# Feed-forward stages 1 to 3 in products of 512 and 384 tokens instead of twice 448

## The chip, the cores and the metric

The kernel runs on one core of a Trainium2 chip. A core has a matrix engine (TensorE, PE in the profile; its weight loads are listed apart as PEld), three engines for elementwise work (VectorE = DVE, ScalarE = ACT, GpSimd = POOL) and a queue engine for transfers (SyncE = SP). They run their own instruction streams and wait for each other by semaphores. The metric is the device time of one execution in microseconds, the median of several.

## The reference

Attention with 2 batches, 12 heads, 448 tokens, head size 64, with a causal mask, and on its output two feed-forward layers with 896 tokens, model width 768 and inner width 2048:

```python
scores = scale * np.matmul(q, k.transpose(0, 1, 3, 2))      # masked above the diagonal, softmax
x = attention_output.transpose(0, 2, 1, 3).reshape(896, 768)
h = x @ w_in;   g = h * np.cos(h);    x = g @ w_out          # layer 1
h = x @ w_in2;  g = gate(h);          out = g @ w_out2       # layer 2
# gate(h): h where h >= 1, 0 where h <= -1, else (h + 1)**2 / 4
```

The weights reach the kernel as 64-bit floats, which it reads as integer words.

## The kernel before, in words

**The four feed-forward products are stages.** Stage 1 is x1 @ w_in, stage 2 is g1 @ w_out, stage 3 is x2 @ w_in2, stage 4 is g2 @ w_out2. Every factor is split into a high and a low part in the format fp32r (`whi`, `wlo`, `x1h`, `x1l`, ...), and each product is the sum of three passes: high by high, low of the activations, low of the weights (`passes`).

**In stages 1 to 3 the weights are stationary and the tokens move.** A matmul loads 128x128 weights into the array and streams tokens past them. All 896 tokens don't fit one matmul, since one writes into one bank of PSUM, 512 fp32 wide. The kernel before streams the two batches apart, 448 tokens each, into a tile `m` of two banks of which it uses the first 448 columns each: `ps[:, b, :S]`.

**A unit** is one piece of weights that is loaded by one DMA, decoded and used: 66 in all. In stage 1 and 3 a unit is a column block of 128 with 6 chunks of the contraction (`c`), so 6 chunks x 2 batches x 3 passes = 36 matmuls (line 442), in the order batch, chunk, pass. In stage 2 an output block takes three units of 5, 5 and 6 chunks (`f`), 30, 30 and 36 matmuls (line 471), in the order chunk, batch, pass. Stage 1 has 16 units, stage 2 has 18, stage 3 has 16. Stage 4 turns the roles round: activations stationary, 384 weight columns moving (line 578), 16 units of 42 matmuls.

**Work beside the matmuls.** `ahead(u)` issues, after the matmuls of unit u, the decode of unit u+2 (lines 143 to 167, on ACT and DVE, the last step writes `wlo`) in turns with the activation of unit u (`act_cos`, lines 353 to 366, in stage 1; `act_gate`, lines 372 to 382, in stage 3; `act_none`, lines 385 and 387, after an output block of stage 2). The activation reads the finished `m` as `[128, 2, 448]` and writes the high and low part of the next stage's factor. Four `m` tiles take turns. Stage 3 begins with five of its six chunks, and only then needs the last block of x2, whose activation runs meanwhile: the first unit sorts its matmuls so that chunk 5 comes last, and runs the rest of the activation (`before`) ahead of it.

**Attention ends before stage 1 does its own.** Parts of units 0 and 1 (60 of their 72 matmuls) fill holes at the end of the attention (`FILL`, `ffn_in_part`). The order on each engine is the order in which the code issues: the schedule is written by hand.

Of the kernel before, what the change touches and what calls it, by code (L numbers as in the profile page):

```python
# [60 lines left out]
def attention_then_two_ffn(  # L61
# [17 lines left out]
    nc = tc.nc  # L79
    B, H, S, D = shape  # L80
    NT, DM = out.shape
    DFF = w_in1.shape[1]
    NP = H // 2
    KD = DM // P
# [18 lines left out]
    def f32(t):  # L103
        return t.bitcast(F32)
# [14 lines left out]
    raws, ready = {}, {}  # L119
# [264 lines left out]
    def act_none(h, xh, xl):  # L384
        nc.scalar.copy(out=xh, in_=h)
        yield
        nc.vector.tensor_tensor(out=xl, in0=h, in1=f32(xh), op=ALU.subtract)


    def joint(t):  # L390
        return t.rearrange("p (b s) -> p b s", b=B)

    def run(gen):
        if gen is not None:
            next(gen, None)
# [4 lines left out]
    def decode(u):  # L400

        if u < len(units):
            if u not in decodes:
                decodes[u] = decode_unit(u)
            run(decodes[u])

    def ahead(u, act=None):

        now, late, work["now"] = work["now"], work["late"], act
        d = u + W_AHEAD
        run(late)
        decode(d)
        run(now)
        run(now)
        decode(d + 1)
        decode(d)
        run(now)
        run(now)  # L420
        decode(d)
        decode(d)
        run(now)
        work["late"] = now

    def passes(w, x):
        return ((w[0], x[0]), (w[0], x[1]), (w[1], x[0]))

    parts = {}

    def ffn_in_part(u, x, b, chunks):

        if u not in parts:
            parts[u] = (new_ps(), ready.pop(u), set())
        ps, w, done = parts[u]
        s = slice(b * S, (b + 1) * S)
        for c in chunks:
            first = not any((b, i) in done for i in range(KD))
            done.add((b, c))
            last = all((b, i) in done for i in range(KD))  # L440
            for t, (l, r) in enumerate(passes(w, x)):
                nc.tensor.matmul(  # L442
                    ps[:, b, :S], l[:, c, :], r[c][:, s], start=(first and t == 0), stop=(last and t == 2)
                )

    def ffn_in(u, x, g, act, before=None):

        for fc in range(KF):
            done = parts[u][2] if u in parts else set()
            left = [(b, c) for b in range(B) for c in range(KD) if (b, c) not in done]  # L450
            if fc == 0:
                left.sort(key=lambda bc: (bc[1] == KD - 1, bc))
            for b, c in left:
                if c == KD - 1 and before:
                    before()
                    before = None
                ffn_in_part(u, x, b, (c,))
            ps = parts.pop(u)[0]
            ahead(u, act(ps[:, :, :S], joint(g[0][fc]), joint(g[1][fc]), u))
            u += 1  # L460

    def ffn_mid(u, g, x):
        for dc in range(KD):
            ps = new_ps()
            for f0, m in MID:
                w = ready.pop(u)
                for f in range(m):
                    for b in range(B):
                        s = slice(b * S, (b + 1) * S)
                        for t, (l, r) in enumerate(passes(w, g)):  # L470
                            nc.tensor.matmul(  # L471
                                ps[:, b, :S], l[:, f, :], r[f0 + f][:, s],
                                start=(f0 + f == 0 and t == 0), stop=(f0 + f == KF - 1 and t == 2),
                            )
                ahead(u)
                u += 1
            last = act_none(ps[:, :, :S], joint(x[0][dc]), joint(x[1][dc]))
            if dc < KD - 1:
                work["now"] = last
        return last  # L480
# [16 lines left out]
    def new_ps():  # L497
        made.append(None)
        return ps_m[(len(made) - 1) % 4].tile([P, 2, 512], F32, tag="s", name=f"m{len(made)}")
# [55 lines left out]
    ps_m += [ps_2, ps_2]  # L555
    g1 = new_g("g1")
    ffn_in(0, x1, g1, act_cos)
    x2 = new_x("x2")
    last = ffn_mid(KF, g1, x2)
    g2 = new_g("g2")  # L560
    u = KF + KD * len(MID)
    ffn_in(u, x2, g2, act_gate, lambda: [run(last), run(last)])
    u += KF


    TB = NT // P
    for e in range(2):
        po = []
        for t in range(0, TB, 2):
            ps = new_ps()  # L570
            po += [ps[:, i, :NO] for i in range(2)]
        for f0 in range(0, KF, 2):
            w = ready.pop(u)
            for t in range(TB):
                s = slice(t * P, (t + 1) * P)
                for f in range(2):
                    for i, (r, l) in enumerate(passes(w, g2)):
                        nc.tensor.matmul(  # L578
                            po[t], l[f0 + f][:, s], r[:, f, :],
                            start=(f0 + f == 0 and i == 0), stop=(f0 + f == KF - 1 and i == 2),  # L580
                        )
            ahead(u)
            u += 1
        for t in range(TB):
            ob = x_p.tile([P, NO], F32, tag=f"x{'hl'[e]}{t % KD}", name=f"ob{e}_{t}")
            if t % 2:
                nc.vector.tensor_copy(out=ob, in_=po[t])
            else:
                nc.scalar.copy(out=ob, in_=po[t])
            nc.sync.dma_start(out=out[t * P : (t + 1) * P, e * NO : (e + 1) * NO], in_=ob)  # L590
# [31 lines left out]
```

## Time and profile before

| | us |
|---|---|
| median of 3 runs | 566.83 (566.78 to 567.08) |
| the profiled execution, as a run | 566.84 |
| its span in the trace | 565.0 |
| stage 1 without fill, from its unit 2: first matmul | 102.55 |
| stage 2 begins | 206.71 |
| stage 3 begins | 325.75 |
| stage 4 begins | 444.79 |
| last matmul of stage 4 begins | 561.10 |

The profiled execution lies on the median, so its rows can be summed against it. The 1.8 us between span and run lie outside the trace.

Matmuls are pipelined: the time that a row gives as the duration of one holds its way through the array, and the next begins long before it ends. What a matmul costs in a stream of its kind is the distance from its start to the start of the next.

### The profile page before, as it was taken

What the parts mean: (1) busy time and instruction counts of PE and PEld (TensorE: products, weight loads), DVE (VectorE), ACT (ScalarE), POOL (GpSimd) and SP (SyncE); (2) the same over time, 40 slices, a digit from 0 to 9 for tenths busy, and PEclk for the clock granted to TensorE, in tenths of its full rate; (3) what the DMA queues carried; (4) which work ended last, traced back from release to release, by engine and by line L of the source; (5) the groups of instructions that cost most, each with busy time, mean ns of one, the idle gap of its engine ahead of it and who ended that gap; (6) DMA issues with size and microseconds to landing.
All of it is one profiled execution on the core that took longest, in us unless ns stands there. A gap on an engine that the chain in (4) does not pass through costs nothing.

```text
span 565.0 us, 8048 instructions
## 1 busy us (share of the span) xinstructions
PE 557.9 (99%) x3105; PEld 495.6 (88%) x3105; DVE 398.7 (71%) x566; ACT 291.7 (52%) x477; POOL 55.1 (10%) x106
## 2 busy tenths in 40 slices
PE   7999999999999999999999999999999999999997
PEld 3666678999999999999999999999999999999997
DVE  5777574699999997654754678888889875547501
ACT  4998883777777773322222245556555622232101
POOL 4657662000000000000000000000000000000000
PEclk9999999999999999999999999999999999999999
DMA  9843011233333324332423523333334343354002
GB/s 311 292 140 98 2 57 33 80 112 113 112 113 102 103 93 150 103 102 94 148 65 104 169 66 105 109 113 111 113 112 113 99 128 114 108 162 160 1 1 98
DMA packets 49254, 62.25 MB, mean 110 GB/s; under 512 B 1856, under 2 KB 43584, under 8 KB 49216
## 3 DMA queue, kind: packets, MB, share of 16 engines
q1 hardware_dynamic: 49072, 61.51, 34.5%
q8 instruction: 24, 0.39, 0.3%
q10 hardware_dynamic: 144, 0.23, 0.1%
q14 instruction: 14, 0.11, 0.1%
HBM read 58.98 MB, written 2.75 MB: 109 GB/s over the span
## 4 chain that ended last, share of the span: by engine, by line
PE 98%; DVE 1%; ACT 0%; issue 0%; POOL 0%; ACTq 0%; POOLq 0%
PE m L442 42%; PE m L471 21%; PE m L578 21%; PE o L334 4%; PE sa L219 2%; PE tx L309 2%; PE sc L206 2%; PE tw L309 1%; PE tz L309 1%; PE sb L219 1%; PE warm L513 1%; DVE nma L247 0%; ACT p L269 0%; PE sa L229 0%; PE sa L232 0%
## 5 line engine op out<-in xcount | busy, mean ns | idle before, releaser
L164 ACT CAST whi<-f 128x768 fp32r<-128x768 f32 (+1 forms) x66 | 54.0, 818 | 119.5 <-DVE f L157 78.5
L167 DVE TENSOR_TENSOR wlo<-f,whi 128x768 fp32r<-128x768 f32 (+1 forms) x63 | 58.4, 928 | 47.7 <-ACT whi L164 47.7
L578 PE MATMUL m<-whi,g2h 128*128 128x384 f32 x224 | 74.8, 334 | 0.0
L578 PE MATMUL m<-wlo,g2h 128*128 128x384 f32 x224 | 74.8, 334 | 0.0
L578 PE MATMUL m<-whi,g2l 128*128 128x384 f32 x224 | 74.8, 334 | 0.0
L442 PE MATMUL m<-x1h,whi 128*128 128x448 f32 x192 | 70.9, 369 | 0.0
L442 PE MATMUL m<-x2l,whi 128*128 128x448 f32 x192 | 70.7, 368 | 0.0
L471 PE MATMUL m<-g1h,wlo 128*128 128x448 f32 x192 | 70.7, 368 | 0.0
L442 PE MATMUL m<-x2h,wlo 128*128 128x448 f32 x192 | 70.7, 368 | 0.0
L471 PE MATMUL m<-g1l,whi 128*128 128x448 f32 x192 | 70.7, 368 | 0.0
L442 PE MATMUL m<-x2h,whi 128*128 128x448 f32 x192 | 70.7, 368 | 0.0
L471 PE MATMUL m<-g1h,whi 128*128 128x448 f32 x192 | 70.7, 368 | 0.0
L442 PE MATMUL m<-x1h,wlo 128*128 128x448 f32 x192 | 70.7, 368 | 0.0
L442 PE MATMUL m<-x1l,whi 128*128 128x448 f32 x192 | 70.6, 368 | 0.0
L143 ACT ACTIVATE f<-raw 128x768 f32<-128x768 f32 (+1 forms) x66 | 58.7, 891 | 20.9 <-DVE wlo L167 20.9
L157 DVE SCALAR_TENSOR_TENSOR f<-raw,f 128x768 uint32<-128x768 uint32 (+1 forms) x66 | 61.8, 936 | 2.3
L154 DVE SCALAR_TENSOR_TENSOR f<-raw,f 128x768 uint32<-128x768 uint32 (+1 forms) x66 | 61.4, 930 | 0.9
L578 PEld LDWEIGHTS m<-whi,g2h 128*128 128x128 f32 x224 | 42.1, 188 | 0.0
L578 PEld LDWEIGHTS m<-whi,g2l 128*128 128x128 f32 x224 | 42.1, 188 | 0.0
L578 PEld LDWEIGHTS m<-wlo,g2h 128*128 128x128 f32 x224 | 42.0, 188 | 0.0
L442 PEld LDWEIGHTS m<-x2l,whi 128*128 128x128 f32 x192 | 36.0, 188 | 3.7
L471 PEld LDWEIGHTS m<-g1h,wlo 128*128 128x128 f32 x192 | 36.0, 188 | 3.7
(91 smaller groups left out, 912.9 us busy)
## 6 DMA issues: line engine op xcount, KB each, us to landing
raw<-in_moe_w_in SPq DMA_DIRECT2D x32, 768.0 KB, 4.5
raw<-in_moe_w_out SPq DMA_DIRECT2D x22, 768.0 KB, 4.4
raw<-in_moe_w_out SPq DMA_DIRECT2D x12, 640.0 KB, 3.8
v<-in_v SPq DMA_DIRECT2D x12, 256.0 KB, 5.0
k<-in_k SPq DMA_DIRECT2D x12, 224.0 KB, 4.7
out<-ob SPq DMA_DIRECT2D x14, 192.0 KB, 1.9
qr<-in_q SPq DMA_DIRECT2D x11, 224.0 KB, 4.9
qr<-in_q ACTq DMA_DIRECT2D x1, 224.0 KB, 3.6
```

Of the source, the lines that this page charges most:

```text
L143: nc.scalar.activation(out=fl, in_=raw.bitcast(F32).rearrange("p (m two) -> p m two", two=2)[:, :m, 1], func=AF.Abs)
L154: nc.vector.scalar_tensor_tensor(out=bits, in0=low, scalar=29, in1=bits, op0=ALU.logical_shift_right, op1=ALU.bitwise_or,)
L157: nc.vector.scalar_tensor_tensor(out=bits, in0=high, scalar=0xC0000000, in1=bits, op0=ALU.bitwise_and, op1=ALU.bitwise_or,)
L164: nc.scalar.copy(out=hi[:, :m], in_=fl)
L167: e.tensor_tensor(out=lo[:, :m], in0=fl, in1=f32(hi)[:, :m], op=ALU.subtract)
L206: nc.tensor.matmul(s[heads(j), :S], self.q[heads(j), FULL * QB :], self.k[heads(j), :], start=True, stop=False)
L219: nc.tensor.matmul(s[:, j, o : o + w], self.q[heads(j), i * QB : w], self.k[heads(j), :w], start=(o == 0), stop=False,)
L309: nc.tensor.transpose(o, i, ident)
L334: nc.tensor.matmul(self.o[heads(j), c * QB : S], self.v[:, j, c, :], self.pT[:, c, j, c * QB :], start=(c == 0), stop=(c == FULL),)
L442: nc.tensor.matmul(ps[:, b, :S], l[:, c, :], r[c][:, s], start=(first and t == 0), stop=(last and t == 2))
L471: nc.tensor.matmul(ps[:, b, :S], l[:, f, :], r[f0 + f][:, s], start=(f0 + f == 0 and t == 0), stop=(f0 + f == KF - 1 and t == 2),)
L578: nc.tensor.matmul(po[t], l[f0 + f][:, s], r[:, f, :], start=(f0 + f == 0 and i == 0), stop=(f0 + f == KF - 1 and i == 2),)
```

## The change

Tokens are no longer cut at the batch border but after 512. A unit of stages 1 to 3 does all its matmuls on one of the two spans, 512 or 384 tokens, and then all on the other; the next unit begins with the span with which the last one ended (`spans.reverse()`). The tile `m` is used flat, columns 0 to 895 over both banks, and read by the activations as two times 448 columns of that. Units 0 and 1, which are begun during the attention, stay with 448. The first unit of stage 3 still keeps chunk 5 for its end, first of the 384 span, then of the 512 span.

```diff
+    spans = [slice(0, 512), slice(512, NT)]
+
+    def flat(ps):
+        return ps.rearrange("p b s -> p (b s)")[:, :NT]
...
     def ffn_in(u, x, g, act, before=None):
         for fc in range(KF):
-            done = parts[u][2] if u in parts else set()
-            left = [(b, c) for b in range(B) for c in range(KD) if (b, c) not in done]
-            if fc == 0:
-                left.sort(key=lambda bc: (bc[1] == KD - 1, bc))
-            for b, c in left:
...
-                ffn_in_part(u, x, b, (c,))
-            ps = parts.pop(u)[0]
-            ahead(u, act(ps[:, :, :S], joint(g[0][fc]), joint(g[1][fc]), u))
+            if u in parts:
+                done = parts[u][2]
+                for b in range(B):
+                    ffn_in_part(u, x, b, [c for c in range(KD) if (b, c) not in done])
+                h = parts.pop(u)[0][:, :, :S]
+            else:
+                h, w = flat(new_ps()), ready.pop(u)
+                left = [(s, c) for s in spans for c in range(KD)]
+                if before:
+                    left = [(s, c) for s in spans for c in range(KD - 1)] + [(s, KD - 1) for s in spans[::-1]]
+                for s, c in left:
...
+                    for t, (l, r) in enumerate(passes(w, x)):
+                        nc.tensor.matmul(
+                            h[:, s], l[:, c, :], r[c][:, s],
+                            start=(c == 0 and t == 0), stop=(c == KD - 1 and t == 2),
+                        )
+                if left[-1][0] is not spans[0]:
+                    spans.reverse()
+                h = joint(h)
+            ahead(u, act(h, joint(g[0][fc]), joint(g[1][fc]), u))
...
     def ffn_mid(u, g, x):
-            ps = new_ps()
+            ps = flat(new_ps())
...
-                for f in range(m):
-                    for b in range(B):
-                        s = slice(b * S, (b + 1) * S)
+                for s in spans:
+                    for f in range(m):
                         for t, (l, r) in enumerate(passes(w, g)):
                             nc.tensor.matmul(
-                                ps[:, b, :S], l[:, f, :], r[f0 + f][:, s],
+                                ps[:, s], l[:, f, :], r[f0 + f][:, s],
...
+                spans.reverse()
                 ahead(u)
-            last = act_none(ps[:, :, :S], joint(x[0][dc]), joint(x[1][dc]))
+            last = act_none(joint(ps), joint(x[0][dc]), joint(x[1][dc]))
```

On PE in the first unit of stage 2 the kernel before issues this; `m_2282` is the sum's tile, `g1h_1382` and `g1h_1383` the high parts of the activations of chunks 0 and 1 (`g1l` the low ones), `whi_2207` and `wlo_2208` the unit's weights:

```order
1063 L471 MATMUL m_2282<-g1h_1382,whi_2207 128x448
1064 L471 MATMUL m_2282<-g1l_1398,whi_2207 128x448
1065 L471 MATMUL m_2282<-g1h_1382,wlo_2208 128x448
1066 L471 MATMUL m_2282<-g1h_1382,whi_2207 128x448
1067 L471 MATMUL m_2282<-g1l_1398,whi_2207 128x448
1068 L471 MATMUL m_2282<-g1h_1382,wlo_2208 128x448
```

And the changed kernel, on PE in the middle of the same unit, where the width changes (chunk 4 is `g1h_1386`):

```order
1075 L489 MATMUL m_2282<-g1h_1386,whi_2207 128x512
1076 L489 MATMUL m_2282<-g1l_1402,whi_2207 128x512
1077 L489 MATMUL m_2282<-g1h_1386,wlo_2208 128x512
1078 L489 MATMUL m_2282<-g1h_1382,whi_2207 128x384
1079 L489 MATMUL m_2282<-g1l_1398,whi_2207 128x384
1080 L489 MATMUL m_2282<-g1h_1382,wlo_2208 128x384
```

The second batch of a chunk, which followed the first at once, has moved behind all chunks of the first span: fifteen matmuls of 512, then fifteen of 384, as many as before.

On PE at the end of the first unit of stage 3 the kernel before has its six matmuls of chunk 5 (`x2h_2275`, `x2l_2281`) in one width:

```order
1669 L442 MATMUL m_3132<-x2h_2275,whi_3048 128x448
1670 L442 MATMUL m_3132<-x2l_2281,whi_3048 128x448
1671 L442 MATMUL m_3132<-x2h_2275,wlo_3049 128x448
1672 L442 MATMUL m_3132<-x2h_2275,whi_3048 128x448
1673 L442 MATMUL m_3132<-x2l_2281,whi_3048 128x448
1674 L442 MATMUL m_3132<-x2h_2275,wlo_3049 128x448
1675 L442 MATMUL m_3183<-x2h_2270,whi_3096 128x448
```

The changed kernel has there:

```order
1669 L471 MATMUL m_3132<-x2h_2275,whi_3048 128x384
1670 L471 MATMUL m_3132<-x2l_2281,whi_3048 128x384
1671 L471 MATMUL m_3132<-x2h_2275,wlo_3049 128x384
1672 L471 MATMUL m_3132<-x2h_2275,whi_3048 128x512
1673 L471 MATMUL m_3132<-x2l_2281,whi_3048 128x512
1674 L471 MATMUL m_3132<-x2h_2275,wlo_3049 128x512
1675 L471 MATMUL m_3183<-x2h_2270,whi_3096 128x512
```

Chunk 5 stands at the same places, 31st to 36th of the unit, and the next unit goes on with 512. Over the whole program 1656 matmuls of 448 have become 828 of 512 and 828 of 384, the width changes 50 times, and the rows of the other engines and of the DMA queues are the same in the same order.

## Rows read from the trace of the kernel before

**Rows 1.** The page: busy time of the engines, and the clock granted to PE.

```profile
PE 557.9 (99%) x3105; PEld 495.6 (88%) x3105; DVE 398.7 (71%) x566; ACT 291.7 (52%) x477; POOL 55.1 (10%) x106
...
PEclk9999999999999999999999999999999999999999
```

**Rows 2.** The page: the chain of work that ended last.

```profile
PE 98%; DVE 1%; ACT 0%; issue 0%; POOL 0%; ACTq 0%; POOLq 0%
PE m L442 42%; PE m L471 21%; PE m L578 21%; PE o L334 4%; PE sa L219 2%; PE tx L309 2%; PE sc L206 2%; PE tw L309 1%; PE tz L309 1%; PE sb L219 1%; PE warm L513 1%; DVE nma L247 0%; ACT p L269 0%; PE sa L229 0%; PE sa L232 0%
```

**Rows 3.** The timeline of PE where stages meet: start us, us, engine, line, operation.

```profile
206.71 0.37 PE L471 MATMUL m<-g1h,whi 128*128 128x448 f32 x1
...
325.75 0.37 PE L442 MATMUL m<-x2h,whi 128*128 128x448 f32 x1
...
444.58 0.37 PE L442 MATMUL m<-x2h,wlo 128*128 128x448 f32 x1
444.79 0.34 PE L578 MATMUL m<-whi,g2h 128*128 128x384 f32 x1
444.97 0.33 PE L578 MATMUL m<-whi,g2l 128*128 128x384 f32 x1
445.14 0.33 PE L578 MATMUL m<-wlo,g2h 128*128 128x384 f32 x1
...
561.10 0.34 PE L578 MATMUL m<-wlo,g2h 128*128 128x384 f32 x1
```

**Rows 4.** The timeline of PE, a burst of fill matmuls between attention's.

```profile
88.30 0.37 PE L442 MATMUL m<-x1l,whi 128*128 128x448 f32 x1
...
89.11 0.37 PE L442 MATMUL m<-x1h,wlo 128*128 128x448 f32 x1
```

**Rows 5.** The timeline of DVE in stage 1: two rounds of the write of `wlo`.

```profile
107.52 0.95 DVE L167 TENSOR_TENSOR wlo<-f,whi 128x768 fp32r<-128x768 f32 x1
...
113.55 1.08 DVE L362 TENSOR_TENSOR ax<-m,ar 128x896 f32<-128x896 f32 x1
114.55 0.95 DVE L167 TENSOR_TENSOR wlo<-f,whi 128x768 fp32r<-128x768 f32 x1
```

**Rows 6.** The timeline of PE: the first matmul of unit 3.

```profile
109.99 0.37 PE L442 MATMUL m<-x1h,whi 128*128 128x448 f32 x1
```

**Rows 7.** The timeline of ACT: reading `m`, and a read of SBUF beside it.

```profile
150.67 0.91 ACT L353 ACTIVATE ax<-m 128x896 f32<-128x896 f32 x1
151.61 0.95 ACT L354 ACTIVATE ar<-ax 128x896 f32<-128x896 f32 x1
```

**Rows 8.** The timeline of DVE: the last low parts of g1 and of x2.

```profile
213.82 1.09 DVE L366 TENSOR_TENSOR g1l<-ax,g1h 128x896 fp32r<-128x896 f32 x1
...
326.89 1.09 DVE L387 TENSOR_TENSOR x2l<-m,x2h 128x896 fp32r<-128x896 f32 x1 [5.10 <-ACT x2h L385]
```

**Rows 9.** Groups of weight loads, 92 to 445 us: count, busy us, mean ns, idle before.

```profile
L471 PEld LDWEIGHTS m<-g1h,whi 128*128 128x128 f32 x192 | 36.0, 188 | 3.5
```

More of the change, by code (lines that the diff above doesn't have):

```diff
@@ L448, in ffn_in @@
         for fc in range(KF):
-            done = parts[u][2] if u in parts else set()
-            left = [(b, c) for b in range(B) for c in range(KD) if (b, c) not in done]
-            if fc == 0:
-                left.sort(key=lambda bc: (bc[1] == KD - 1, bc))
-            for b, c in left:
-                if c == KD - 1 and before:
-                    before()
-                    before = None
-                ffn_in_part(u, x, b, (c,))
-            ps = parts.pop(u)[0]
-            ahead(u, act(ps[:, :, :S], joint(g[0][fc]), joint(g[1][fc]), u))
+            if u in parts:
[9 more added lines that the diff above has]
+                for s, c in left:
+                    if c == KD - 1 and before:
+                        before()
+                        before = None
+                    for t, (l, r) in enumerate(passes(w, x)):
[7 more added lines that the diff above has]
+            ahead(u, act(h, joint(g[0][fc]), joint(g[1][fc]), u))
             u += 1
```

## The prediction

> **What bounds the kernel now.** First the page's busy times and the clock. PE is busy 99% of the span at its higher level, 2.4 GHz, from end to end [rows 1]. The chain that ended last is 98% PE; lines 442, 471 and 578, the four feed-forward stages, hold 84% of the span [rows 2]. So a nanosecond off each matmul of stages 1 to 3 comes off the end, as long as nobody else gets late. What one costs has to be read from starts, not from durations (0.37 us each, overlapping). Between the stage borders of the timeline [rows 3] lie:
> - stage 2: 576 matmuls of 448 in 325.75 - 206.71 = 119.04 us, 206.67 ns each; stage 3: 576 in 444.79 - 325.75 = 119.04 us, the same. No wait is in either: two stages with different engines busy beside them agree to the nanosecond.
> - stage 4: 671 steps of 384 columns in 561.10 - 444.79 = 116.31 us, 173.3 ns each.
>
> At one column per cycle of 2.4 GHz these would be 186.67 and 160.0 ns. So a matmul of 448 pays 20.0 ns over its columns, one of 384 pays 13.3 ns. The change lives on what one of 512 pays.
>
> **The change, part by part.**
>
> *The widths.* 1656 matmuls of 448 become 828 of 512 and 828 of 384; columns, weight loads and count stay. A pair costs 2 x 206.67 = 413.33 ns before. After it costs P(384) + P(512). For P(384) the nearest row is stage 4's 173.3 ns: same format, same 128x128 weight load, though there the activations are stationary. With it, break-even is P(512) = 240.0 ns. No row has a 512 of this format, so I bound it:
> - Low: the 13.3 ns of the 384 is a fixed price, and the 448 pays 6.7 more for being no whole number of 128 columns. P(512) = 213.33 + 13.3 = 226.7 ns; the pair saves 13.3 ns.
> - Middle: the price grows in steps, 13.3 for 3 x 128 columns, 20.0 for anything above 384. P(512) = 213.33 + 20.0 = 233.3 ns; the pair saves 6.67 ns. The three prices would be 2, 3 and 3 times 6.67 ns, one for each border between blocks of 128 columns that the stream passes. The same value comes from adding 64 columns at the clock, 26.67 ns, to the nearest row, the 448.
> - High: the straight line through both rows, (206.67 - 173.33)/64 = 0.521 ns a column, gives 206.67 + 33.33 = 240.0 ns and no gain. Above it, if the price grows by half each 64 columns (13.3, 20, 30), stand 243.3 ns and a loss of 3.3 ns a pair.
>
> I take the middle: 448 is the nearest row in width and in the roles of the operands. One row says that the 20 ns are not rigid: in a short burst between attention's matmuls the same form took (89.11 - 88.30)/4 = 202.5 ns [rows 4]. So part of the price is a phase between weight load and stream and not the stream itself; from there P(512) would be 202.5 + 26.67 = 229.2, between low and middle. Gain: 828 x 6.67 = 5.52 us.
>
> *The changes of width.* There are 50 instead of the one at stage 4's door. That one shows its price: the first 384 after a 448 lasted 444.97 - 444.79 = 0.18 us against 0.173 in the stream [rows 3], some 6 ns. 49 x 6 = 0.3 us to pay; bounds 0 and 0.6. Had the widths alternated from matmul to matmul, 1656 such changes would have cost 9.9 us; grouped, this term is small whatever the direction.
>
> *The weight loads.* A load is listed with 188 ns [rows 9], longer than 173 ns. Stage 4 streams 384 columns behind each load at 173.3 all the same, so a short matmul does hide a load, and its price is in the row. Nothing added.
>
> *Cover on DVE in stage 1.* DVE is the tightest neighbour. Its round lasts 114.55 - 107.52 = 7.03 us there [rows 5], and PE's unit 36 x 206.67 = 7.44 us. Unit 3's `wlo` is ready at 107.52 + 0.95 = 108.47 and first wanted at 109.99 [rows 6]: 1.52 us to spare, growing by 0.41 a unit. After, the unit takes 18 x 406.67 = 7.32 us, at the low bound 7.20: the reserve still grows, by 0.29 or 0.17. Cost nothing. In stages 2 and 3 the reserve is larger.
>
> *Reading `m` flat.* The activations now read two times 448 columns across the bank border. Reading `m` takes ACT 0.91 us, a like operation on SBUF 0.95 [rows 7]: 896 elements set the time, no bank shows. Zero; 0.1 us more for each of the two DVE readings would make the DVE round 7.23, still under 7.32.
>
> *The order inside a unit.* In the third unit of stage 2, chunk 15 of g1 is wanted after 15 matmuls rather than 30. Its low part ends at 214.91 [rows 8]; the unit begins near 219.1 in the old trace (60 matmuls after 206.71) and wants it at 222.2. Seven microseconds of room. The last block of x2 ends at 326.89 + 1.09 = 327.98 [rows 8] and is wanted 30 matmuls into stage 3: before at 325.75 + 6.20 = 331.95, after 6.10 instead of 6.20 behind the door, 3.9 us of room. Both zero; should either cover go, it would be paid once.
>
> **Sum.** 566.84 - 5.52 + 0.29 = 561.6 us. The profiled execution is on the median, so this stands for the median too.
>
> **Rivals.**
>
> *The price is a straight line, or a price of the place.* Then cutting 896 columns as 512 + 384 or 448 + 448 is the same. Two mechanisms lead there: 0.521 ns a column throughout; or 20 ns for every matmul of stages 1 to 3 because the weights are stationary, so that 384 costs 160 + 20 = 180 there and 512 costs 233.3, 413.3 together. For: two points always lie on a line, and stage 4 differs in operands too. Against: a stream cannot pay more per column than the clock asks without some border or limit, and a limit of 0.521 ns a column would forbid the 173.3 of the 384, which is 0.451 a column. Time: 566.84 + 0.29 = 567.1.
> The Trainium skill, "TensorE: Matmul & The Clock Gate", section "Back-to-back issue gap", has such a law: columns over 2.4 GHz and 2.5 ns a matmul. By it the pair costs 378.3 ns either way and the change is worth nothing; the trace does not agree with its sizes, since it has 206.7 and 173.3 where the rule says 189.2 and 162.5, and an excess that is not constant.
>
> *The 512 is as cheap as the 384.* P(512) = 226.7: 566.84 - 11.04 + 0.29 = 556.1. For: both are whole multiples of 128 columns. Against: it makes 448 the odd one on no other evidence.
>
> *Slower: the price climbs.* Going from 384 to 448 it rose by half. If it does so again, P(512) = 243.3 and the change costs 828 x 3.33 = 2.76, with the changes of width 3.05: 569.9. It decides from P(512) = 240 on, and reaches over the noise at 241. For: the bent course fits both rows as well as the step. Against: no resource in the trace fills up with width (PSUM's bank is just filled, not passed).
>
> *It doesn't do what it says* would mean other widths; the issue order has 828 and 828, so I leave it at nothing.
>
> **How the numbers follow.** Forecast (P(512) from 229 to 237, time 558.0 to 564.6): 0.43. Straight line or place (237 to 241): 0.24. As cheap as the 384 (under 229): 0.20. Climbing price: 0.13. What a measurement of this kernel can tell from no change is about 0.2%, 1.1 us. Faster by more than that means P(512) under 238.3: the forecast, the cheap case and little of the second, 0.64; within 0.2%: 0.23; slower: 0.13. The range goes from the cheap case, 555.8, to the straight line with its changes of width, 567.3, and leaves out the climbing price and the lower tail. The likeliest case alone: 558.0 to 564.6.
>
> **What would show it.** In the profile after: starts of the 512 matmuls 233 ns apart, of the 384 ones 173 apart; stages 2 and 3 at 288 x 406.67 = 117.1 us each rather than 119.04; stage 1's units at 7.32; stage 4 unchanged at 116.3 after its first matmul; one matmul in each unit some 6 ns longer where the width changes; no idle PE. The forecast is wrong if the 512 stand 240 or more apart, if the 384 of these stages stand 180 apart, or if PE waits for DVE in stage 1.

## The result, and the profile after

The changed kernel takes 557.55 us (median of 4 runs, 557.48 to 557.68) against 566.82 before: ratio 0.9836, 95% interval 0.9819 to 0.9853. It is faster by 9.3 us; 5.2 were forecast. Its profiled execution took 557.5 us with a span of 555.7, so it lost 9.3 of span too.

The page after, busy times and the chain that ended last (line 471 is now stages 1 and 3, line 489 stage 2, line 597 stage 4, line 449 what is left in 448):

```profile
PE 548.1 (99%) x3105; PEld 484.3 (87%) x3105; DVE 398.5 (72%) x566; ACT 291.8 (53%) x477; POOL 55.3 (10%) x106
...
PE 98%; DVE 1%; ACT 0%; issue 0%; POOL 0%; ACTq 0%; POOLq 0%
PE m L471 39%; PE m L597 21%; PE m L489 21%; PE o L334 4%; PE m L449 3%; PE sa L219 2%; PE tx L309 2%; PE sc L206 2%; PE tw L309 1%; PE tz L309 1%; PE sb L219 1%; PE warm L532 1%; DVE nma L247 0%; ACT p L269 0%; PE sa L229 0%
```

PE still bounds the kernel at 98% of the chain, as in [rows 1, 2]; the busy times of DVE, ACT and POOL moved by 0.2 us at most. The timeline of PE after, at the first matmul of unit 2 and at the stage borders of [rows 3]:

```profile
102.58 0.40 PE L471 MATMUL m<-x1h,whi 128*128 128x512 f32 x1
...
203.89 0.39 PE L489 MATMUL m<-g1h,whi 128*128 128x512 f32 x1
...
319.69 0.39 PE L471 MATMUL m<-x2h,whi 128*128 128x512 f32 x1
...
435.45 0.33 PE L597 MATMUL m<-whi,g2h 128*128 128x384 f32 x1
...
551.76 0.34 PE L597 MATMUL m<-wlo,g2h 128*128 128x384 f32 x1
```

Stage 2 takes 115.80 us instead of 119.04, stage 3 115.76 instead of 119.04, stage 4 116.31 as before. Stage 1 from its unit 2 takes 101.31 (102.58 to 203.89) instead of 104.16. That is 2.85 + 3.24 + 3.28 = 9.37 us, the whole gain.

A pair costs 115.80 us / 288 = 402.1 ns. What it is made of shows at a change of width. The timeline of PE in stage 2, the first change towards 384 and the next towards 512:

```profile
206.61 0.39 PE L489 MATMUL m<-g1h,whi 128*128 128x512 f32 x1
...
207.29 0.33 PE L489 MATMUL m<-g1h,whi 128*128 128x384 f32 x1
...
207.81 0.35 PE L489 MATMUL m<-g1h,whi 128*128 128x384 f32 x1
208.00 0.34 PE L489 MATMUL m<-g1l,whi 128*128 128x384 f32 x1
...
208.53 0.33 PE L489 MATMUL m<-g1l,whi 128*128 128x384 f32 x1
...
212.52 0.39 PE L489 MATMUL m<-g1h,whi 128*128 128x512 f32 x1
212.75 0.40 PE L489 MATMUL m<-g1l,whi 128*128 128x512 f32 x1
212.98 0.40 PE L489 MATMUL m<-g1h,wlo 128*128 128x512 f32 x1
...
214.60 0.39 PE L489 MATMUL m<-g1h,whi 128*128 128x512 f32 x1
```

The last three 512 ahead of the change stand (207.29 - 206.61) / 3 = 0.227 us apart; over all settled ones in the trace it is 226.67 ns. The 384 settle at 173.33. Behind the change the distances sway: the first seven 384 take 208.53 - 207.29 = 1.24 us instead of 7 x 173.33 = 1.21, the first nine 512 take 214.60 - 212.52 = 2.08 instead of 2.04. Then the stream is steady. Summed from single starts in ns, over 24 changes of each kind, a change towards 384 costs 25.8 ns, spread over the next six distances, and one towards 512 costs 40.8, spread over nine: 33.3 on average. (The expectations below put them at 27, 41 and 34.) The one change of the kernel before, from 448 to 384 where stage 4 begins at 444.79 [rows 3], had no such sway: twelve matmuls on, its timeline of PE has

```profile
446.88 0.33 PE L578 MATMUL m<-whi,g2h 128*128 128x384 f32 x1
```

which is 2.09 us later, where 12 x 173.33 ns is 2.08. In single starts the first distance is 6 ns longer and the next are settled.

So the gain is 828 x (413.33 - 400.0) = 11.04 us, less 50 x 33.3 ns = 1.67: 9.37 us, the sum over the stages. 566.84 - 9.37 = 557.5, the profiled time.

The cover on DVE, to be compared with [rows 5, 6] (timeline of DVE in stage 1, then PE's first matmul of unit 3):

```profile
107.55 0.95 DVE L167 TENSOR_TENSOR wlo<-f,whi 128x768 fp32r<-128x768 f32 x1
...
114.58 0.95 DVE L167 TENSOR_TENSOR wlo<-f,whi 128x768 fp32r<-128x768 f32 x1
```

```profile
109.85 0.33 PE L471 MATMUL m<-x1h,whi 128*128 128x384 f32 x1
```

DVE's round is still 7.03 us, PE's unit now 7.24, and unit 3's weights are ready 109.85 - 108.50 = 1.35 us early. The reserve grows by 0.2 a unit. The profile lists no wait of PE from 75 us to the end.

### The profile page after: what moved, and what is told of

It reads as the page before. It is cut to its first block, busy times and chain, and to the rows that moved or that the text cites. A ratio compares the mean times of both kernels' runs of the same rounds, so it can differ in the third digit from the quotient of the medians.

```text
span 555.7 us, 8048 instructions
## 1 busy us (share of the span) xinstructions
PE 548.1 (99%) x3105; PEld 484.3 (87%) x3105; DVE 398.5 (72%) x566; ACT 291.8 (53%) x477; POOL 55.3 (10%) x106
## 4 chain that ended last, share of the span: by engine, by line
PE 98%; DVE 1%; ACT 0%; issue 0%; POOL 0%; ACTq 0%; POOLq 0%
PE m L471 39%; PE m L597 21%; PE m L489 21%; PE o L334 4%; PE m L449 3%; PE sa L219 2%; PE tx L309 2%; PE sc L206 2%; PE tw L309 1%; PE tz L309 1%; PE sb L219 1%; PE warm L532 1%; DVE nma L247 0%; ACT p L269 0%; PE sa L229 0%
## 5 line engine op out<-in xcount | busy, mean ns | idle before, releaser
L489 PE MATMUL m<-g1h,wlo 128*128 128x512 f32 (+1 forms) x192 | 69.7, 363 | 0.0
L471 PE MATMUL m<-x2h,wlo 128*128 128x512 f32 (+1 forms) x192 | 69.7, 363 | 0.0
L489 PE MATMUL m<-g1l,whi 128*128 128x512 f32 (+1 forms) x192 | 69.6, 363 | 0.0
L471 PE MATMUL m<-x2l,whi 128*128 128x512 f32 (+1 forms) x192 | 69.6, 363 | 0.0
L471 PE MATMUL m<-x2h,whi 128*128 128x512 f32 (+1 forms) x192 | 69.5, 362 | 0.0
L489 PE MATMUL m<-g1h,whi 128*128 128x512 f32 (+1 forms) x192 | 69.5, 362 | 0.0
L471 PE MATMUL m<-x1h,wlo 128*128 128x512 f32 (+1 forms) x168 | 61.0, 363 | 0.0
L471 PE MATMUL m<-x1l,whi 128*128 128x512 f32 (+1 forms) x168 | 60.9, 363 | 0.0
L471 PE MATMUL m<-x1h,whi 128*128 128x512 f32 (+1 forms) x168 | 60.8, 362 | 0.0
L471 PEld LDWEIGHTS m<-x2h,whi 128*128 128x128 f32 x192 | 36.1, 188 | 3.9
```

The costliest lines, as they stand in the source:

```text
L471: nc.tensor.matmul(h[:, s], l[:, c, :], r[c][:, s], start=(c == 0 and t == 0), stop=(c == KD - 1 and t == 2),)
L489: nc.tensor.matmul(ps[:, s], l[:, f, :], r[f0 + f][:, s], start=(f0 + f == 0 and t == 0), stop=(f0 + f == KF - 1 and t == 2),)
```

## The experiments

Two theories stand after the result. *Settling*: a stream of matmuls with a weight load before each falls into a steady distance, here called its course, that depends on the width; 448 happens to fall into a dear one (20.0 ns over its columns), 512 and 384 into a cheap one (13.3), and each change unsettles it for a while. *Whole blocks*: widths that are multiples of 128 are cheap, all others dear. Beside them: that the order in a unit has a part in the gain, and that a change has a fixed price.

**Order without width** (grouped448). All of one span, then all of the other, as the changed kernel, with 448 and 448:

```diff
-    spans = [slice(0, 512), slice(512, NT)]
+    spans = [slice(0, S), slice(S, NT)]
...
-        return ps.rearrange("p b s -> p (b s)")[:, :NT]
+        return ps[:, :, :S]
...
-                                ps[:, s], l[:, f, :], r[f0 + f][:, s],
+                                ps[:, s.start // S], l[:, f, :], r[f0 + f][:, s],
```

> The changed kernel's order (all of one span, then all of the other, the next unit beginning with the last span) with the widths of before, 448 and 448. If the gain is the width's alone, the time is that of the kernel before, 566.8, and the starts stay 206.67 ns apart. If the order has a part in it (a weight load or a bank that the same span again and again serves faster), it falls towards 557.6.

566.86 us against 566.87, ratio 1.0003 (0.9994 to 1.0013). The timeline of PE has stage 2 from here to here:

```profile
206.72 0.37 PE L489 MATMUL m<-g1h,whi 128*128 128x448 f32 x1
...
325.76 0.37 PE L471 MATMUL m<-x2h,whi 128*128 128x448 f32 x1
```

119.04 us, as before to 10 ns. The order alone does nothing; the gain is the widths'.

**More changes of width** (no_reverse). Every unit begins with the 512 span, 96 changes instead of 50:

```diff
-                if left[-1][0] is not spans[0]:
-                    spans.reverse()
...
-                spans.reverse()
                 ahead(u)
```

> The changed kernel, but every unit begins with the 512 span: 96 changes of width instead of 50. Theory 'settling' (each change unsettles the next 6 to 9 matmuls, 27 ns in all towards 384 and 41 ns towards 512): 46 more changes at 34 ns, 1.6 us, 559.1 us. Rival, the prediction's 6 ns a change: 557.8. Rival, changes are free and the longer matmuls at a span's start wait for something else at a unit's start (weights, a bank): no difference, 557.6.

558.99 us, ratio to before 0.9868 (0.9853 to 0.9883): 1.44 us over the changed kernel, 31 ns for each of the 46 changes more. Settling said 34; the prediction's 6 ns falls for changes so far apart, and so does that they are free.

**Changes after every third matmul** (every3), the span inside the chunk, 552 changes (the two `spans.reverse()` go too):

```diff
-                left = [(s, c) for s in spans for c in range(KD)]
+                left = [(s, c) for c in range(KD) for s in spans]
...
-                for s in spans:
-                    for f in range(m):
+                for f in range(m):
+                    for s in spans:
...
```

> The changed kernel with the span inside the chunk, as the batch was in stage 2 before: three matmuls of 512, three of 384, 552 changes of width. Without any change of width the time would be near 557.55 - 1.7 = 555.9. Theory 'settling', each change begins the same course anew (229, 234, 236; 171, 175, 178, so 23 ns over six matmuls): 276 x 23 = 6.3 us, 562.2. Rival, a fixed 34 ns a change: 18.8 us, 574.6, slower than before. Rival, 6 ns a change: 559.2.

562.21 us, ratio to before 0.9925 (0.9908 to 0.9941). A fixed 34 ns a change (574.6) is out; the forecast from the first three distances after a change, 562.2, is met in time, though not in its mechanism: a change does not begin the same course anew. The groups alternate; in the trace's single starts three 512 take 229, 233, 236 ns in one group and 233, 236, 224 in the next, three 384 take 168, 178, 185 and then 175, 174, 175. Over such a round of twelve matmuls this comes to 23.6 ns per six where the forecast had 23, so the agreement in time is in part luck. In the timeline of PE, six pairs between the first 384 of one group and of the group two further on:

```profile
250.12 0.33 PE L487 MATMUL m<-g1h,whi 128*128 128x384 f32 x1
...
251.35 0.34 PE L487 MATMUL m<-g1h,whi 128*128 128x384 f32 x1
...
252.57 0.33 PE L487 MATMUL m<-g1h,whi 128*128 128x384 f32 x1
```

2.45 us / 6 = 408 ns a pair, between the 402.1 of the changed kernel and the 413.3 of before.

**The width alone, by itself** (law). Behind the changed kernel's last output a stream of the same kind, which nothing uses:

```diff
+    probe = new_ps()
+    for n in (512, 496, 480, 464, 456, 448, 440, 432, 416, 400, 384, 352, 320, 288, 256, 192, 128):
+        for i in range(24):
+            nc.tensor.matmul(probe[:, i % 2, :n], g2[0][i % 8][:, :P], g2[1][i % 8][:, :n], start=True, stop=True)
...
+    for i in range(48):
+        n = 512 if i % 2 == 0 else 384
...
```

> The changed kernel, and behind its last output a stream of 648 more matmuls of the same format (three-pass factors, 128x128 weights, a load before each), 24 of each width from 512 down to 128 columns, then 448 from other start columns and into other PSUM columns, 512 from column 32, then 512 and 384 in turns singly and by threes; their sums are used by nothing. It reads the start-to-start distance of each width in one stream. Theory 'whole blocks': what a matmul pays over its columns at 2.4 GHz is 13.3 ns for a multiple of 128 columns and 20.0 ns for any other width: 512 at 226.7, 384 at 173.3, 256 at 120.0, and 448 at 206.7, 480 at 220.0, 416 at 193.3, 320 at 153.3. Theory 'place': 20.0 ns belongs to where 448 tokens start (byte 1792 of a row) or to the half-used bank: then 448 from column 64, or into columns 64 to 511, falls to 200.0 and 480, 416, 320 pay 13.3. Theory 'settling': 206.7 is a phase into which a stream of 448 locks; the widths between show prices without a pattern in 128, some below 13.3. The turns: by threes 226.7 + 173.3 and some 8 ns a pair more (first three after a change in the stages: 229, 234, 236 and 171, 175, 178); singly either 400 a pair (the first after a change is 229 and 171) or, if every change costs a fixed 34 ns, 468.

The stream has 600 matmuls, not the 648 that the expectation counts; like the two appended streams further on it was executed once. Windows of PE from the first start of one width's 24 matmuls to the first start of the next, in the order 496, 480, 464, 448, 440, 416, 400, 384, 320, 288, 256, 128 columns (first the window and its length; the counts include one to three that reach in):

```profile
556.21:561.49 5.28, 5.28 (x26) 4.50 (x25) 1.00 0.00 0
561.49:566.69 5.20, 5.20 (x26) 4.50 (x25) 1.00 0.00 0
566.69:571.73 5.04, 5.04 (x26) 4.50 (x25) 1.00 0.00 0
576.71:581.66 4.95, 4.95 (x26) 4.51 (x24) 1.00 0.01 3
581.66:586.46 4.80, 4.80 (x25) 4.51 (x24) 1.00 0.00 0
591.16:595.68 4.52, 4.52 (x25) 4.49 (x24) 1.00 0.00 0
595.68:600.01 4.33, 4.33 (x26) 4.33 (x25) 1.00 0.00 0
600.01:604.19 4.18, 4.18 (x25) 4.18 (x25) 1.00 0.02 4
608.05:611.57 3.52, 3.52 (x26) 3.52 (x25) 1.00 0.00 0
611.57:614.73 3.16, 3.16 (x26) 3.16 (x25) 1.00 0.00 0
614.73:617.61 2.88, 2.88 (x27) 2.88 (x26) 1.00 0.00 0
620.27:622.92 2.65, 2.65 (x26) 2.65 (x24) 1.00 0.00 0
```

Length over 24, less columns over 2.4 GHz; where the start of a window still settles, the mean of its last twelve:

| columns | ns apart | over the columns |
|---|---|---|
| 512 | 226.7 | 13.3 |
| 496 | 220.0 | 13.3 |
| 480 | 216.7 | 16.7 |
| 464 | 210.0 | 16.7 |
| 448 | 206.7 | 20.0 |
| 440 | 200.0 | 16.7 |
| 416 | 188.3 | 15.0 |
| 400 | 180.0 | 13.3 |
| 384 | 173.3 | 13.3 |
| 320 | 146.7 | 13.3 |
| 288 | 131.7 | 11.7 |
| 256 | 120.0 | 13.3 |
| 128 | 111.7 | 58.3 |

Of the widths left out, 456 pays 18.9, 432 14.8 and 352 14.5, and 192 stands 111.7 ns apart like 128. Each width ran once here, behind the next wider one; what ran before can matter, as the run history shows.

The timeline of PE further on, sections merged: 448 from column 448 of the row; 512 from column 32; 448 into PSUM column 64; 512 and 384 in turns:

```profile
627.93 5.12 PE L618 MATMUL m<-g2l,g2h 128*128 128x448 f32 x24
632.89 5.73 PE L620 MATMUL m<-g2l,g2h 128*128 128x512 f32 x24
638.46 5.04 PE L622 MATMUL m<-g2l,g2h 128*128 128x448 f32 x24
643.33 10.07 PE L625 MATMUL m<-g2l,g2h 128*128 128x512 f32 x48
```

Whole blocks falls: 496, 400 and 320 are no multiples of 128 and pay 13.3. There is no straight line and no climb either: the price rises on both sides towards 448, the dearest width apart from the narrow 192 and 128. Settling is met where it said that some widths pay below 13.3: 288 does. Place falls too: 448 from column 448 takes (632.89 - 627.93) / 24 = 206.7, and from column 64 it settles there as well. One 448, the last, settled at 202.4 and one 512, from column 32, at 232.6, which the next runs took up. 512 and 384 in turns took 238 and 176 ns.

**In turns, in the kernel** (every1): the span inside the pass, in stage 2 in the same way.

```diff
-                    for t, (l, r) in enumerate(passes(w, x)):
+                    for t, (l, r), s in [(t, lr, s) for t, lr in enumerate(passes(w, x)) for s in spans]:
```

> The changed kernel with the span inside the pass: 512 and 384 in turns, matmul by matmul, 1656 changes of width. From the appended stream of the run law, where 512 and 384 in turns took 238 and 176 ns: 828 x (413.4 - 402.1) = 9.4 us more than the changed kernel, 566.9 us, so the whole gain is gone and the time is that of the kernel before. Rival, the prediction's 6 ns a change: 555.9 + 9.9 = 565.8. Rival, 34 ns a change whatever the group: 612.

566.79 us against 566.81, ratio 1.000 (0.999 to 1.001). The whole gain is gone, as forecast from the appended stream. The timeline of PE has a 512 and a 384 merged in each row:

```profile
249.98 0.58 PE L487 MATMUL m<-g1h,wlo 128*128 128x512 f32 x2
...
251.64 0.57 PE L487 MATMUL m<-g1h,whi 128*128 128x512 f32 x2
```

Four pairs in 1.66 us are 415 ns each; over all of stage 2 it is 413.4: what 448 and 448 cost. Written in this order, the same change would have been called worthless. The price of one change of width thus falls the closer the changes stand: 33 ns in the changed kernel, 11.4 in groups of three ((562.21 - 555.9) / 552), 6.6 in turns ((566.79 - 555.9) / 1656).

**Where the operands stand** (places), another appended stream, `mm(i, bank, columns, from column, into PSUM column)`:

```diff
+    for i in range(24):
+        nc.tensor.matmul(**mm(i, i % 2, 512, 64, 0))
...
+    for i in range(90):
+        nc.tensor.matmul(**(mm(i, 1, 512, 384, 0) if i // 15 % 2 else mm(i, 0, 384, 0, 128)))
```

> The changed kernel and an appended stream that nothing uses, 24 matmuls each: 512 from columns 0, 64, 128, 256 and 384 of the moving row, 384 from column 512 and into PSUM columns 128 and 64, 448 into PSUM columns 0, 16, 32 and 64, and twice 90 matmuls in groups of 15: 512 from column 0 and 384 from 512 (as the changed kernel) and 384 from column 0 into PSUM columns 128 to 511, 512 from 384 (the other way to cut). In the run law a 512 from column 32 took 232.6 instead of 226.7, and a 448 into PSUM columns 64 to 511 took 202.4 instead of 206.7. Theory 'settling' (the price is a phase, and the place of an operand moves it like the width does): more such places show, without order in 128 columns, and the groups of 15 cost another sum after a change than the 27 and 41 ns. Rival 'whole blocks of 512 byte': starts at 0, 128, 256 and 384 stay at 226.7, and only 64 (like 32) falls out.

The timeline of PE, sections merged: 512 from column 64, 128, 256, 384; 384 (the next start); 448 into PSUM column 64; groups of 15 as in the changed kernel; groups of 15 cut the other way:

```profile
563.10 5.60 PE L624 MATMUL m<-g2l,g2h 128*128 128x512 f32 x24
568.54 5.60 PE L626 MATMUL m<-g2l,g2h 128*128 128x512 f32 x24
573.98 5.60 PE L628 MATMUL m<-g2l,g2h 128*128 128x512 f32 x24
579.42 5.60 PE L630 MATMUL m<-g2l,g2h 128*128 128x512 f32 x24
584.86 4.35 PE L632 MATMUL m<-g2l,g2h 128*128 128x384 f32 x24
...
612.24 5.12 PE L644 MATMUL m<-g2l,g2h 128*128 128x448 f32 x24
617.20 18.37 PE L646 MATMUL m<-g2l,g2h 128*128 128x512 f32 x90
635.41 18.34 PE L648 MATMUL m<-g2l,g2h 128*128 128x384 f32 x90
```

Each 512 section is 5.44 us / 24 = 226.7 ns, wherever it starts among these. 448 into column 64 takes 4.96 / 24 = 206.7, so the 202.4 of the run law was not the PSUM column alone. The other way to cut gives the same groups to 0.03 us. My expectation that more such places would show was wrong; so was the rival's, since 64 did not fall out.

**What came before** (history), a third appended stream with the edit of the last (`mm` with other columns, in the order that the expectation gives).

> The changed kernel and an appended stream that nothing uses, 24 or 48 matmuls a section: 512 from column 0, 32, 0, 16 of the moving row; 448 from 0, from 32; 512, 448; 384 from 32; 448; 320; 448; 512 from 32; 448; 512. In the run law one 512 from column 32 took 232.6 and the 448 after it 202.4; starts at 64, 128, 256 and 384 took 226.7 in the run places. Theory 'place': a start at 32 or 16 always gives 232.6 for 512, whatever came before, and every 448 from column 0 gives 206.7. Theory 'memory': the stream keeps a phase from what came before; then a 512 from 32 behind a 512 from 0 stays at 226.7, and 448 gives 206.7 or 202.4 by its forerunner.

The timeline of PE: 512 from column 32; from 0; from 16; 448; and further on 448 behind 320; 512 from 32; 448; 512:

```profile
557.37 5.75 PE L622 MATMUL m<-g2l,g2h 128*128 128x512 f32 x24
562.97 5.62 PE L624 MATMUL m<-g2l,g2h 128*128 128x512 f32 x24
568.42 5.67 PE L626 MATMUL m<-g2l,g2h 128*128 128x512 f32 x24
573.93 5.04 PE L628 MATMUL m<-g2l,g2h 128*128 128x448 f32 x24
...
611.56 5.03 PE L642 MATMUL m<-g2l,g2h 128*128 128x448 f32 x24
616.42 5.74 PE L644 MATMUL m<-g2l,g2h 128*128 128x512 f32 x24
622.00 10.07 PE L646 MATMUL m<-g2l,g2h 128*128 128x448 f32 x48
631.91 5.65 PE L648 MATMUL m<-g2l,g2h 128*128 128x512 f32 x24
```

Both theories get half. A start at 32 is dear each time, 5.60 / 24 = 233.3 and 5.58 / 24 = 232.5, one at 16 takes 229.6: place counts. And 448 from column 0 takes 4.88 / 24 = 203.3 and 4.86 / 24 = 202.5 here, but 9.91 / 48 = 206.5 behind the second 512 from 32, and 206.7 in the stages: memory counts. A stream of 448 from column 0 has two steady courses, 206.7 and 202.4, and kept the one it fell into as long as it lasted: 24 matmuls in the cheap one, a whole stage of 576 in the dear one. The bursts of [rows 4] were in the second; their single distances, 203, 199, 207, 203 ns, are those of the 202.4 course. What picks the course, and why 448 has a dear one at all, these runs don't show. It is not the section before alone: behind a 512 from column 32 the 448 fell to 202.4 in the run law (into PSUM column 64) and to 206.7 here.

No version better than the changed kernel followed. Its 50 changes cost 1.7 us; even an order that halved them would bring 0.85 us, and the cheap widths 496 and 400 cost 220.0 + 180.0 = 400.0 ns, the same pair price, and would start one span at column 496 or 400, an odd multiple of 16, where the 512 from 16 paid 3 ns. Neither was tried. Nor were the stages run with 448 in its cheap course: a pair would cost 2 x 202.4 = 404.8 ns there, an estimate from the appended streams. By it 8.5 of the 13.3 ns that a pair saves come from leaving the dear course of 448, and 4.8 would be left against the cheap one.

## Why the prediction came out as it did

The time lies inside the stated range and just below the likeliest case, 558.0 to 564.6. What happened is the case that was given 0.20.

- *What bounds*: right. PE alone; every microsecond off its stream came off the end. (The granted clock was 1.00 in every stage, as read; "from end to end" is not quite so, it was 0.98 on average in the first 81.8 us.)
- *P(384) = 173.3 ns*: right to 0.1 ns once settled, although the roles of the operands differ between the stages. The rival "price of the place" falls with it.
- *P(512)*: the step that failed, in size. I took the middle, 233.3, because "448 is the nearest row in width and in the roles of the operands". The 512 stands at 226.7, the low bound. The 448's 20.0 ns was not a step that holds above 384 but belongs to 448 and the widths beside it, and a row that pointed there was shown: the burst at 202.5 [rows 4] had the same form at another distance. The prediction read it as a sign that the 20.0 is not rigid and still built on it; it could have moved the weight to the 384, the other row without sign of such a thing. That the price is "a phase between weight load and stream" no run shows; shown is that the same 448 has two steady distances. The term measured 11.04 us where 5.52 was put.
- *Why low*: the low bound's reason, a multiple of 128, was wrong as well. 496, 400 and 320 pay the same 13.3.
- *The changes of width*: the right sign, too small. The 6 ns were read rightly for the one change in the trace, from 448 to 384. What failed is to carry them over to changes between 512 and 384, which sway for six to nine distances and cost 33.3 ns each, 1.67 us instead of 0.29. For widths in turns, 9.9 us were put and 10.9 measured. But a single change is cheapest there and dearest in groups; "grouped, this term is small" holds only because the changes are few.
- The two misses partly cancelled, which is luck: 11.04 - 1.67 = 9.37 against 5.52 - 0.29 = 5.2. With the wider gain and changes at 6 ns the time would have been 556.1.
- *Weight loads, DVE's cover, reading `m` flat, the order inside a unit*: each at nothing, each confirmed: no wait of PE, DVE's round unchanged at 7.03, its reserve growing by 0.2 a unit, 0.92 us for ACT's reading of `m` where it was 0.91 [rows 7].
- *Rivals*: "as cheap as the 384" is what happened, at 0.20; its 556.1 lacked only the dearer changes. The climbing price and the straight line are refuted by the pair at 400.0 ns and by the run law. The rule of the Trainium skill that the prediction names beside the straight line is given in that section for an isolated matmul, and this stream has a load before each.
- *The range*: its upper end, 567.3, is 0.2 above the 567.1 that the terms for the straight line give; nothing hangs on it.

## What to carry to other kernels

In a stream of matmuls with a load before each, measure the distance between starts for the widths in question; it is not linear in the width, and a stream of the candidate width, appended behind the kernel, gives it in one run, though a width can have more than one course, as 448 had. Keep matmuls of one width together: with the same widths, groups of 18 to 36 gained 9.3 us, groups of 15 to 21 7.9, groups of three 4.7, and in turns nothing. A change of width read at one pair of widths does not price another pair. When the same instruction shows two distances in one trace, don't carry either over to another width.

## What the runs showed of the hardware

- At 2.4 GHz, with this format and a 128x128 load before each matmul, the widths measured from 256 to 512 pay 11.7 to 16.7 ns over their columns, but 456 pays 18.9 and 448 20.0 or 15.7 by its history.
- Settled distances are often whole steps of 6.67 ns: 18 for 256, 22 for 320, 26 for 384, 27 for 400, 31 for 448, 33 for 496, 34 for 512.
- Below about 192 columns the distance stops falling: 111.7 ns for 192 and for 128 columns alike. The Trainium skill, "TensorE: Matmul & The Clock Gate", section "LDWEIGHTS (loading the stationary operand)", puts a load at its columns over 1.2 GHz, 106.7 ns for 128; the floor agrees within 5 ns, though the traces list a load with 188 to 192 ns. That the load sets the floor is not shown, since no run varies it.
- A 512 that starts at column 32 or 16 of its row takes 233 or 229 to 230 ns; from 0, 64, 128, 256 or 384 it takes 226.7. In the run history a 384 from column 32 took 175.8 instead of 173.3.
- A change between 512 and 384 costs 25.8 ns towards 384 and 40.8 towards 512 when the next one is 15 or more matmuls away; the one from 448 to 384 cost 6.
